# A second PSUM bank for the filler matmuls, and Mish as four products of 1024 columns

## The chip, the core and the metric

One core of one Trainium2 chip runs the whole program. The metric is device time in microseconds from launch to end. Before the change it is 889.89 us, the median of three runs (887.64 to 893.85).

## What is computed

The reference is one block with two branches over the same 2048 x 640 input, mixed by a gate per row (bfloat16 in and out):

```python
def _A_ref(x, wqkv, wo):                      # 32 heads of 20 columns
    q, k, v = ...                             # x @ wqkv
    scores = einsum("bhqd,bhkd->bhqk", q, k) * 20 ** -0.5
    o = einsum("bhqk,bhkd->bhqd", softmax(scores), v)
    return o @ wo
def _B_ref(x, w1, b1, w2):                    # 640 -> 1536 -> 640
    h = x @ w1 + b1
    return (h * tanh(softplus(h))) @ w2       # Mish
g = sigmoid((x * gate_w).sum(-1, keepdims=True))
return g * _A_ref(x, ...) + (1 - g) * _B_ref(x, ...)
```

The work that sets the scale is the exponential of 32 x 2048 x 2048 scores.

## The kernel before, in words

The kernel is a program that plans its own instruction streams. `attention()` walks through steps; at each step it appends instructions to a list, and each engine (TensorE, called pe; ScalarE, act; VectorE, dve; GpSimd, pool; SyncE, sp) later runs its part of that list in order, with semaphores where one waits for another. A planner's clock with costs such as `EXP`, `WIDE`, `PASS` decides what fits where; the order is fixed before the chip runs.

**Steps.** The scores are cut into 2048 blocks of 128 keys x 512 queries (the last group of one quarter of the queries in two halves of 256). A step handles a slot of up to three blocks. TensorE writes them into three of the eight PSUM banks: even steps into banks 0 to 2, odd steps into banks 3 to 5 (`scores(s)`). The score matmuls (L1045) use 32 rows of the array each, so the two or three of one step run beside one another and cost one pass of 512 columns. ScalarE then takes the exponential of the whole slot in one instruction (`emit_e`, L1068) from PSUM into `ETS`. In many steps the third block goes to VectorE instead: `choose` hands it over, `emit_x` (L1099) forms an int16 whose bits are an approximate fp16 exponential, and three shaded copies (L1119) are made of each finished tile of four blocks, so that each such tile is summed from four shades. ScalarE's instruction then covers only two blocks (1024 columns). The scores of step s+2 are issued while ScalarE is at step s+1 (`emit_s(step + 2)`), and need the banks that step s has left.

**Value products.** Four finished blocks are multiplied with V (L1224), four matmuls beside one another, accumulating in bank 6 (`ACC`); a group ends with a copy to `OUNG` and a division by the sums that goes through a DRAM round trip (L1295 to L1305, L1265).

**Fillers.** All other matmuls are tasks: keys, queries and values (L536 to L711), the bound on the scores (L752), the hidden layer (`h_task`, L829), its output (`b_task`, L900), the output projection (`p_task` and `part_task`, L924). `pick` takes the next task whose inputs are ready, `put` issues one of its matmuls at a time, at most up to the planned end of ScalarE's instruction (`limit` in the main loop), and all use bank 7 (`FB`): a new task waits until VectorE has emptied the bank of the one before. What has not found a place by the last step is issued after it.

**Mish.** Pairs of finished hidden tiles (1024 columns) go to ScalarE for a tanh (L863) and then to VectorE in twelve pieces (L879 to L893): a square, a sum, a product, a product of halves, a reciprocal (L883), and products with it. The pieces lie in a queue (`blend`) and are slipped in wherever `work` finds room on VectorE.

**The end.** After the last step the remaining fillers run, then eight last projections of the last 256 queries (`late_mm`), their mixing and the stores.

## Time and profile before

| | before |
|---|---|
| median of 3 runs | 889.89 us (887.64 to 893.85) |
| the profiled execution's own time | 890.57 us |
| its span, first to last instruction | 888.0 us |
| TensorE busy (matmul rows) | 774.3 us, 87% |
| ScalarE busy | 799.7 us, 90% |
| VectorE busy | 734.8 us, 83% |
| mean granted TensorE clock | 0.981 of full speed |

The page has a busy sum for each engine, the span in forty slices, the chain of work that ended last, and groups of instructions with what ended the idle time before them. Busy is the union of an engine's rows: a matmul's row goes on after the next one may start, so a busy TensorE is not one without room. The time of one step of a pipelined engine is therefore read from start to start in the rows in order of time.

### The profile page before, as it was taken

The numbers are of one execution on the slowest core, as the hardware profiler recorded it, in microseconds if no ns is written. First come the engines' busy times: TensorE is split into PE (matmuls) and PEld (weight loads), VectorE is DVE, ScalarE is ACT, GpSimd is POOL, SyncE is SP. The second block draws the span as 40 slices with busy tenths as digits, with TensorE's granted clock in tenths as the row PEclk, the third lists the DMA queues.
The fourth block names the chain that finished last, engine by engine and source line by source line (L and its number), as shares of the span: only waits on it lengthen the run. The fifth ranks groups of instructions, "written<-read, shape, count | busy, mean of one in ns | idle before, by whom it ended". The sixth has DMA issues, their size and how long they took to land.

```text
span 888.0 us, 17316 instructions
## 1 busy us (share of the span) xinstructions
PE 774.3 (87%) x7304; PEld 275.8 (31%) x7304; DVE 734.8 (83%) x1232; ACT 799.7 (90%) x714; POOL 16.4 (2%) x29
## 2 busy tenths in 40 slices
PE   7887898989899888979999989889999899888874
PEld 3333233223432223212223323333333333333332
DVE  4785787799978889988789888999999989878753
ACT  6987987999789997969999999999999999999930
POOL 2000000000000000000000000000000000000000
PEclk9998999999999999979999999999999999999997
DMA  9012010001112211121111112111011202111101
GB/s 215 19 43 61 29 55 16 13 28 53 52 37 72 65 45 44 44 65 47 42 45 34 40 54 66 44 43 54 18 36 50 77 14 72 50 44 51 35 12 34
DMA packets 70021, 42.57 MB, mean 48 GB/s; under 512 B 20616, under 2 KB 65920, under 8 KB 69888
## 3 DMA queue, kind: packets, MB, share of 16 engines
q1 hardware_dynamic: 67568, 40.89, 16.4%
q8 instruction: 60, 0.98, 0.5%
q10 hardware_dynamic: 2256, 0.47, 0.3%
q0 software_dynamic: 112, 0.01, 0.1%
q14 instruction: 25, 0.20, 0.1%
HBM read 33.97 MB, written 5.23 MB: 44 GB/s over the span
## 4 chain that ended last, share of the span: by engine, by line
ACT 73%; PE 14%; DVE 6%; DMA 6%; issue 1%; SPq 0%
ACT ETS L1068 71%; PE PS L1224 4%; PE PS L1045 3%; DMA KT<-KS 3%; DMA KS<-LN 2%; PE PS L536 2%; ACT REG L863 2%; PE PS L924 1%; DVE LN L1099 1%; PE PS L711 1%; PE PS L900 1%; DVE LN L1119 1%; PE PS L590 1%; DMA LN<-in_A_x_dram 1%; DMA SUMS<-RR 1%
## 5 line engine op out<-in xcount | busy, mean ns | idle before, releaser
L1068 ACT ACTIVATE ETS<-PS 128x1536 bf16<-128x1536 f32 (+1 forms) x683 | 783.3, 1418 | 46.3 <-PE PS L1045 38.9
L1045 PE MATMUL PS<-QT,KT 32*128 32x512 bf16 (+1 forms) x2146 | 271.0, 380 | 83.3 <-ACT ETS L1068 62.8
L1099 DVE TENSOR_SCALAR LN<-PS 128x512 int16<-128x512 f32 x276 | 185.9, 684 | 33.1 <-PE PS L1045 30.8
L1224 PE MATMUL PS<-ETS,V_all 128*21 128x512 bf16 (+1 forms) x1764 | 168.8, 380 | 0.1
L1045 PEld LDWEIGHTS PS<-QT,KT 32*128 32x128 bf16 x2146 | 67.6, 91 | 296.4 <-ACT ETS L1068 267.3
L1119 DVE TENSOR_SCALAR LN<-LN 128x2048 int16<-128x2048 int16 x163 | 107.8, 682 | 2.9 <-PE PS L1224 2.8
L1224 PE MATMUL PS<-LN,V_all 128*21 128x512 f16 x1132 | 98.8, 390 | 0.6 <-DVE LN L1119 0.6
L900 PE MATMUL PS<-W2R,HB 128*128 128x320 bf16 x384 | 72.5, 302 | 2.5 <-DVE XB L907 2.4
L1224 PEld LDWEIGHTS PS<-ETS,V_all 128*21 128x21 bf16 x1764 | 42.6, 90 | 77.2 <-issue 68.5
L829 PE MATMUL PS<-XB,REG 128*128 128x256 bf16 x360 | 56.2, 275 | 1.4 <-DVE OUTT L930 0.7
L924 PE MATMUL PS<-WOQ,QT 128*128 128x320 bf16 x256 | 50.3, 310 | 8.0 <-DVE W2R L930 5.2
L536 PE MATMUL PS<-XB,WOQ 128*128 128x512 bf16 x155 | 45.3, 391 | 1.9 <-DVE HB L839 0.8
L900 PEld LDWEIGHTS PS<-W2R,HB 128*128 128x128 bf16 x384 | 30.1, 97 | 38.8 <-issue 25.2
L839 DVE TENSOR_TENSOR HB<-PS,B1F 128x512 bf16<-128x512 f32 x48 | 33.0, 687 | 11.0 <-PE PS L829 10.4
L883 DVE RECIPROCAL T<-T 128x256 f32<-128x256 f32 x24 | 41.9, 1744 | 0.1
L829 PEld LDWEIGHTS PS<-XB,REG 128*128 128x128 bf16 x360 | 29.0, 97 | 28.2 <-issue 26.0
L1224 PEld LDWEIGHTS PS<-LN,V_all 128*21 128x21 bf16 x1132 | 22.4, 90 | 42.8 <-issue 24.7
L548 DVE CAST QT<-PS 128x512 bf16<-128x512 f32 x31 | 21.3, 686 | 14.4 <-PE PS L536 14.1
L924 PEld LDWEIGHTS PS<-WOQ,QT 128*128 128x128 bf16 x256 | 20.3, 99 | 34.3 <-issue 13.2
L1295 DVE COPY OUNG<-PS 128x512 f32<-128x512 f32 x31 | 21.2, 684 | 8.1 <-PE PS L1224 7.9
L1585 ACT ACTIVATE LN<-PS,GATE 128x320 f32<-128x320 f32 x1 | 0.5, 528 | 29.4 <-PE PS L924 29.4
L863 ACT ACTIVATE REG<-HB 128x1024 f32<-128x1024 bf16 x18 | 25.4, 1413 | 0.0
(123 smaller groups left out, 607.9 us busy)
## 6 DMA issues: line engine op xcount, KB each, us to landing
REG<-in_B_w_dram SPq DMA_DIRECT2D x36, 320.0 KB, 3.2
BCT<-SUMS SPq DMA_DIRECT2D x31, 256.0 KB
W2R<-in_B_w_dram SPq DMA_DIRECT2D x12, 320.0 KB, 4.8
KT<-KS SPq DMA_DIRECT2D x28, 128.0 KB
KS<-LN SPq DMA_DIRECT2D x16, 128.0 KB, 2.5
W2R<-in_B_w_dram SPq DMA_DIRECT2D x1, 1920.0 KB, 8.6
out_dram<-OUTT SPq DMA_DIRECT2D x24, 80.0 KB, 1.6
REG<-in_A_wqkv_dram SPq DMA_DIRECT2D x2, 700.0 KB, 8.5
```

Of the source, the lines that this page charges most:

```text
L536: return lambda e, bank: e.matmul(PS[:, bank, :], pads[:, b, f, :], xt(c)[:, f, :], start=(f == 0), stop=(f == NFT - 1))
L829: return lambda e, bank: e.matmul(PS[:, bank, i * HW:(i + 1) * HW], w1b(n1)[:, f, i * P:(i + 1) * P], xt(c)[:, f, cols], start=(f == 0), s ...
L839: ev = dve(lambda e: e.tensor_tensor(hb, PS[:, bank, :].rearrange("p (i t) -> p i t", i=2), bias, ALU.add), [last, *b1f, *guarded, *b_read ...
L863: ex = pl.add("act", lambda e: e.activation(U, h, AF.Tanh, scale=0.5), [ev, u_free[0]], cost=0.95)
L883: piece(RECIP, lambda e: e.reciprocal(T1[:, :], T1[:, :]))
L900: return lambda e, bank: e.matmul(PS[:, bank, 0:HALF], HB[:, hc % 2, f, t * P:(t + 1) * P], W2[:, f, half * HALF:(half + 1) * HALF], start ...
L924: return lambda e, bank: e.matmul(PS[:, bank, 0:HALF], otn(c, g)[:, t * P:(t + 1) * P], WOG[:, g, half * HALF:(half + 1) * HALF], start=(g ...
L1045: op = pl.add("pe", lambda e, i=i, g=real(g), tile=tile, j=j, cols=cols, c=c, of_q=of_q: e.matmul(scores(s)[:, i, cols], KT[32 * j:32 * j ...
L1068: e_op[s] = pl.add("act", lambda e: e.activation(ETS[:, s % NETS, 0:n, :], scores(s)[:, 0:n, :], AF.Exp, scale=SCALE), [s_op[s], pv_slot.g ...
L1099: ev_op[s] = tile["op"] = dve(lambda e: e.tensor_scalar(dst, scores(s)[:, 2, :], SCALE * ULPS, BASE, ALU.mult, ALU.add), [s_op[s], *tile[" ...
L1119: op = pl.add("dve", lambda e: e.tensor_scalar(to, src, SHADES[n], None, ALU.add), [last, *deps], cost=SHADE)
L1224: lasts[n] = pl.add("pe", lambda e, tile=tile, h=real(g) * HG + j, j=j, src=src[:, cols], of_q=of_q, begin=begin, end=end: e.matmul(PS[32 ...
```

## The change

1. `lend()`: from step 2 on, while the planner's filler rate is above `LEND`, an odd step's slot holds two blocks instead of three (`compose`, `n = SLOT - ...`), and its third bank, 5, is lent to the fillers as `SECOND`. `home()` takes for each new task the one of banks 7 and 5 that came free first. No block goes to VectorE in such a step (`choose` is not asked).
2. The number of steps is no longer fixed; the loop runs until all blocks are done, and due times go by the share of blocks issued (`now["at"]`).
3. `limit` is raised by `OVER` = 0.233: a filler may end that much after the planned end of ScalarE's instruction.
4. Mish: tanh with a bias (`BEND`, from a column of `MXR`), then four products of 1024 columns, without reciprocal. `U2` doubles, `T1` goes, `OUTT` moves into `REG`.
5. Some twenty constants of the planner are other numbers; the tasks' due times end 83 slots before the last instead of 45.

The diff, cut to this:

```diff
-SLACK = 0.3
-LATER = 0.9
+SLACK = 0.21
+LATER = 0.616
...
-END = 45
-SHIFT = 0.4
+END = 83
+SHIFT = 0.492
...
-                ex = pl.add("act", lambda e: e.activation(U, h, AF.Tanh, scale=0.5), [ev, u_free[0]], cost=0.95)
+                G = U2[:, :]
+                ex = pl.add("act", lambda e: e.activation(U, h, AF.Tanh, bias=MXR[:, 3:4], scale=0.5),
+                            [ev, u_free[0], m_bias], cost=0.95)
...
-                piece(RECIP, lambda e: e.reciprocal(T1[:, :], T1[:, :]))
...
+                a, b, c = QUART
+                piece(BROAD, lambda e: e.scalar_tensor_tensor(G, U, a, U, ALU.add, ALU.mult))
+                piece(BROAD, lambda e: e.scalar_tensor_tensor(U, U, 1.0, h, ALU.add, ALU.mult))
+                piece(BROAD, lambda e: e.scalar_tensor_tensor(G, G, b, G, ALU.add, ALU.mult))
+                piece(BROAD, lambda e: e.scalar_tensor_tensor(h, G, c, U, ALU.add, ALU.mult), done)
...
+            n = SLOT - (s % 2 and now["lent"])
             if extra:
-                slots[s] = [order.popleft(), order.popleft(), extra]
+                slots[s] = [order.popleft() for _ in range(min(n - 1, len(order)))] + [extra]
             else:
-                slots[s] = [order.popleft() for _ in range(min(SLOT, len(order)))]
+                slots[s] = [order.popleft() for _ in range(min(n, len(order)))]
+            now["at"] = (len(units) - len(order)) // SLOT - 2
...
+        def lend():
+
+            if now["open"] and now["home"] == SECOND:
+                return
+            want = fast and now["step"] > 1 and now["rate"] > LEND
+            if want and not now["lent"]:
+                s = now["step"]
+                bank_free[SECOND] = ev_op[s] if s in off else e_op[s] if len(slots[s]) == SLOT else bank_free.get(SECOND)
+            now["lent"] = want
...
+        def home():
+
+            some = [FB, SECOND] if now["lent"] else [FB]
+            return min(some, key=lambda n: bank_free[n].t1 if bank_free.get(n) is not None else 0.0)
...
-            limit = pl.now["act"] + (EXP_PAIR if fast and step + 1 in off else EXP) + HOP if step < NSLOT else 1e9
+            limit = pl.now["act"] + wide(step + 1) + HOP + OVER if busy else 1e9
```

What the change moves, at three places.

TensorE in the middle of the loop, about where the first output projections are placed (L1045, now L1048: scores; L1224, now L1242: value products; L924, now L925, and L829, now L840: fillers). Before:

```order
L1045 MATMUL PS<-QT,KT 128x512 x3
L924 MATMUL PS<-WOQ,QT 128x320 x3
L1045 MATMUL PS<-QT,KT 128x512 x3
L1224 MATMUL PS<-ETS,V_all 21x512 x4
L924 MATMUL PS<-WOQ,QT 128x320
L1045 MATMUL PS<-QT,KT 128x512 x3
```

The same stretch of the changed program:

```order
L1048 MATMUL PS<-QT,KT 128x512 x3
L840 MATMUL PS<-XB,REG 128x256
L925 MATMUL PS<-WOQ,QT 128x320 x3
L1048 MATMUL PS<-QT,KT 128x512 x2
L1242 MATMUL PS<-ETS,V_all 21x512 x4
L925 MATMUL PS<-WOQ,QT 128x320
L1048 MATMUL PS<-QT,KT 128x512 x3
```

Every second score set has two matmuls instead of three, and one task's last matmul is followed at once by the next task's first (an L840, then L925), in the other bank. Over the whole program there are 817 score sets instead of 683 and 797 value sets instead of 773; the fillers are the same (546,640 columns of moving data in all); and the stream changes from one of the three kinds (score, value, filler) to another 1883 times instead of 1574, 573 of them from filler to score instead of 454.

TensorE at the end of the program. Before, from the last score set on:

```order
L1045 MATMUL PS<-QT,KT 128x256 x4
L924 MATMUL PS<-WOQ,QT 128x320 x4
L1224 MATMUL PS<-ETS,V_all 21x256 x8
L900 MATMUL PS<-W2R,HB 128x320 x5
L1224 MATMUL PS<-ETS,V_all 21x256 x8
L900 MATMUL PS<-W2R,HB 128x320 x43
L924 MATMUL PS<-WOQ,QT 128x320 x56
L1481 MATMUL PS<-KT 128x512
L924 MATMUL PS<-WOQ,QT 128x320 x8
```

The changed program, from its last score set on (L1506 is an idle pass that no result uses):

```order
L1048 MATMUL PS<-QT,KT 128x256 x6
L1242 MATMUL PS<-ETS,V_all 21x256 x8
L925 MATMUL PS<-WOQ,QT 128x320 x2
L1242 MATMUL PS<-ETS,V_all 21x256 x16
L1506 MATMUL PS<-KT 128x512 x5
L925 MATMUL PS<-WOQ,QT 128x320 x8
```

The 43 and 56 filler matmuls that followed the last value set stand ahead of it now; behind it are only the eight last projections and idle passes.

VectorE, one Mish pass among its other work. Before, its later half:

```order
L883 RECIPROCAL T<-T 128x256
L1119 TENSOR_SCALAR LN<-LN 128x2048
L839 TENSOR_TENSOR HB<-PS,B1F 128x512
L884 TENSOR_TENSOR U<-U,T 128x512
L1119 TENSOR_SCALAR LN<-LN 128x2048
L888 TENSOR_TENSOR REG<-REG,U 128x256 x2
L891 SCALAR_TENSOR_TENSOR REG<-REG,U 128x256
L839 TENSOR_TENSOR HB<-PS,B1F 128x512
L891 SCALAR_TENSOR_TENSOR REG<-REG,U 128x256
L892 SCALAR_TENSOR_TENSOR HB<-REG,HB 128x512
L893 SCALAR_TENSOR_TENSOR HB<-REG,HB 128x512
```

The changed program, from a pass's second product to its fourth (L1117: a block's approximate exponential; L1137: a shade):

```order
L892 SCALAR_TENSOR_TENSOR REG<-REG,HB 128x1024
L1137 TENSOR_SCALAR LN<-LN 128x2048
L1117 TENSOR_SCALAR LN<-PS 128x512
L1320 RECIPROCAL RR<-RR 128x16
L893 SCALAR_TENSOR_TENSOR U<-U 128x1024
L1117 TENSOR_SCALAR LN<-PS 128x512
L1137 TENSOR_SCALAR REG<-LN 128x2048
L908 TENSOR_SCALAR XB<-PS,OMG 128x320
L1117 TENSOR_SCALAR LN<-PS 128x512
L894 SCALAR_TENSOR_TENSOR HB<-U,REG 128x1024
```

There are 24 passes in both; a pass has four instructions of 1024 columns instead of twelve of 256 to 1024. VectorE now takes 380 blocks instead of 348 (L1117) and makes 285 shades instead of 261 (L1137). ScalarE has 34 exponentials of 1536 columns and 783 of 1024, before 334 and 349. The DMA issues keep their number and kinds.

## Rows read from the trace of the kernel before

**Rows 1.** Page: busy us of each engine, share of the span, instructions.
```profile
PE 774.3 (87%) x7304; PEld 275.8 (31%) x7304; DVE 734.8 (83%) x1232; ACT 799.7 (90%) x714; POOL 16.4 (2%) x29
```

**Rows 2.** Windows: stretch, busy of each engine (instructions), clock, DMA share, GB/s.
```profile
10.00:450.00 440.00, 386.00 (x3760) 133.62 (x3754) 361.50 (x609) 394.06 (x361) 11.26 (x19) 0.97 0.18 49
450.00:852.00 402.00, 360.92 (x3387) 128.62 (x3385) 356.42 (x591) 401.79 (x348) 0.00 (x0) 1.00 0.16 45
852.00:888.00 36.00, 20.34 (x121) 10.19 (x121) 11.70 (x23) 0.88 (x2) 0.86 (x1) 0.86 0.08 23
```

**Rows 3.** Waits of ScalarE, 10 to 450 us: total us, times, longest.
```profile
ACT ETS L1068 <- PE PS L1045: 38.9, 35, 2.9
ACT ETS L1068 <- PE PS L1224: 6.7, 2, 3.5
```

**Rows 4.** Timeline at the end: start us, us, engine, line, names, count, idle.
```profile
843.87 8.48 ACT L1068 ACTIVATE ETS<-PS 128x1536 bf16<-128x1536 f32 x6
...
854.35 0.42 DVE L1288 TENSOR_TENSOR QT<-PS,BCT 128x256 bf16<-128x256 f32 x1
...
855.29 1.80 PE L900 MATMUL PS<-W2R,HB 128*128 128x320 bf16 x12 [1.14 <-DVE XB L907]
...
880.19 2.34 PE L924 MATMUL PS<-WOQ,QT 128*128 128x320 bf16 x8
```

**Rows 5.** Timeline of ScalarE, 768.41 to 782 us.
```profile
768.41 12.52 ACT L1068 ACTIVATE ETS<-PS 128x1536 bf16<-128x1536 f32 x9
780.39 1.48 ACT L863 ACTIVATE REG<-HB 128x1024 f32<-128x1024 bf16 x1
781.34 1.88 ACT L1068 ACTIVATE ETS<-PS 128x1536 bf16<-128x1536 f32 x1
```

**Rows 6.** Timeline of ScalarE, 303.6 to 309 us.
```profile
303.14 5.69 ACT L1068 ACTIVATE ETS<-PS 128x1024 bf16<-128x1024 f32 x6
308.56 1.20 ACT L863 ACTIVATE W2R<-HB 128x1024 f32<-128x1024 bf16 x1
```

**Rows 7.** Timeline, 606 to 610.4 us, TensorE.
```profile
608.29 0.39 PE L1045 MATMUL PS<-QT,KT 32*128 32x512 bf16 x3 [0.20 <-ACT ETS L1068]
...
608.62 0.40 PE L1224 MATMUL PS<-LN,V_all 128*21 128x512 f16 x4
...
608.84 0.39 PE L1224 MATMUL PS<-REG,V_all 128*21 128x512 f16 x4
...
609.16 0.50 PE L829 MATMUL PS<-XB,REG 128*128 128x256 bf16 x3
...
609.64 0.39 PE L1045 MATMUL PS<-QT,KT 32*128 32x512 bf16 x3
```

**Rows 8.** Groups of VectorE by shape: names, shapes, count, busy us, mean ns, idle.
```profile
L1099 DVE TENSOR_SCALAR LN<-PS 128x512 int16<-128x512 f32 x276 | 185.9, 684 | 33.1 <-PE PS L1045 30.8
L1119 DVE TENSOR_SCALAR LN<-LN 128x2048 int16<-128x2048 int16 x163 | 107.8, 682 | 2.9 <-PE PS L1224 2.8
L883 DVE RECIPROCAL T<-T 128x256 f32<-128x256 f32 x24 | 41.9, 1744 | 0.1
...
L879 DVE SCALAR_TENSOR_TENSOR REG<-REG 128x1024 f32<-128x1024 f32 x18 | 21.9, 1216 | 2.1 <-ACT REG L863 2.1
...
L888 DVE TENSOR_TENSOR REG<-REG,U 128x256 f32<-128x256 f32 x36 | 15.1, 419 | 0.5
...
L892 DVE SCALAR_TENSOR_TENSOR HB<-REG,HB 128x512 bf16<-128x512 f32 x18 | 12.3, 685 | 0.2
```

**Rows 9.** Waits of TensorE, 10 to 450 us: total us, times, longest.
```profile
PE PS L1045 <- ACT ETS L1068: 29.0, 97, 1.1
PE PS L1045 <- DMA KT<-KS: 7.2, 5, 3.7
```

**Rows 10.** Windows around the first fall of the clock.
```profile
78.00:82.00 4.00, 0.42 (x5) 0.22 (x6) 0.98 (x2) 1.08 (x1) 0.00 (x0) 1.00 0.77 187
82.00:86.00 4.00, 3.42 (x42) 2.11 (x46) 2.78 (x5) 2.40 (x2) 0.00 (x0) 0.54 0.06 14
```

More of the change, by code (lines that the diff above doesn't have):

```diff
@@ L342, in attention @@
         acts = deque()
-        now = {"step": -1, "open": None, "bank": False, "rate": 9.0}
+        now = {"step": -1, "at": -2, "open": None, "home": FB, "bank": False, "rate": 9.0, "lent": False}
         if fast:
@@ L387, in later, with dve @@
             at.setdefault(step, []).append(fn)
-        def dve(fn, deps=(), cost=0.1, kind="F"):
+        def dve(fn, deps=(), cost=0.1, kind="F", slack=SLACK):
             ready = max([pl.now["dve"], *(d.t1 + HOP for d in deps if d is not None)])
-            work(ready + (LATER if fast and now["rate"] < BUSY and now["bank"] else SLACK))
+            work(ready + (LATER if fast and now["rate"] < BUSY and now["bank"] else slack))
             return pl.add("dve", fn, deps, cost=cost, kind=kind)
@@ L1424, in pick @@
             for t in tasks:
-                if begin + t.cost > limit or passed and t.due > now["step"] + EAGER:
+                if begin + t.cost > limit or passed and t.due > now["at"] + EAGER:
                     return None
@@ L1456, in room @@
         def room():
[L1458 removed]
+            step = now["at"]
             if step < start:
@@ L1493, in fill_up @@
                     spin(FB, free)
-                elif short and not idle and step + 2 < NSLOT and pl.now["pe"] + PASS + TAIL["pe"] + HOP <= upto:
+                elif short and not idle and step + 2 in slots and pl.now["pe"] + PASS + TAIL["pe"] + HOP <= upto:
                     repeat_s(step + 2)
@@ L1499, in attention @@
         owed = 0.0
-        for step in range(NSLOT + 40):
+        step = -1
+        while True:
+            step += 1
             now["step"] = step
-            if step >= NSLOT and not queue and not tasks and not any(k >= step for k in at):
-                break
-            for t in [t for t in tasks if t.forced and t.due <= step]:
+            assert step < 1500, (len(order), len(tasks), len(queue))
+            if not order and step not in slots:
+                now["at"] = max(now["at"] + 1, NSLOT)
+                if not queue and not tasks and not any(k >= step for k in at):
+                    break
+            for t in [t for t in tasks if t.forced and t.due <= now["at"]]:
                 while now["open"] not in (None, t):
@@ L1513, in attention @@
                 load_w2()
-            if acts and safe(acts[0][0]) < pl.now["act"] and mish_free():
+            if acts and (safe(acts[0][0]) < pl.now["act"] and mish_free() or step not in slots and u_free[0] != "busy"):
                 acts.popleft()[1]()
@@ L1517, in attention @@
             rate = behind = 0.0
-            lag = max((step - t.due for t in tasks if not t.forced and t.ready() is None), default=0)
+            lag = max((now["at"] - t.due for t in tasks if not t.forced and t.ready() is None), default=0)
             for t in tasks:
-                slack = max(1, t.due - AHEAD * t.forced - step)
+                slack = max(1, t.due - AHEAD * t.forced - now["at"])
                 ahead += t.left()
@@ L1526, in attention @@
             now["rate"] = rate
-            if step + 2 < NSLOT:
-                able = step >= CALM and (step < slot_of(0, 1, 0) or behind < CATCH_UP and lag < LAG and room())
-                compose(step + 2, choose(step + 2, able) if fast else None)
+            if order:
+                able = now["at"] >= CALM and (now["at"] < slot_of(0, 1, 0) or behind < CATCH_UP and lag < LAG and room())
+                if step % 2:
+                    lend()
+                compose(step + 2, choose(step + 2, able) if fast and not (step % 2 and now["lent"]) else None)
                 emit_s(step + 2)
@@ L1550, in attention @@
                 fn()
-            work(pl.now["act"] + 0.5 if step < NSLOT else 1e9)
+            work(pl.now["act"] + 0.5 if busy else 1e9)
         assert not queue and not tasks and not bg and not soon and not norm and not tile_now[0] and not blend and not acts, (len(queue), len(tasks), len(bg), len(acts))
```

106 lines of the change are left out of this document (54 added, 52 removed).

## The prediction

> **What bounds the kernel now.** I read the busy sums first [rows 1]: ScalarE 799.7, TensorE 774.3, VectorE 734.8 us of 888, so no average names a bound. The table of stretches does [rows 2]. From 450 to 852 us ScalarE is busy 401.79 of 402 us: there the exponentials are the bound, and nothing else matters. From 10 to 450 us it is busy 394.06 of 440, and the table of its waits says for whom it stood: 45.6 us, nearly all for a score matmul [rows 3]. From 852 us on it does nothing (0.88 us), and neither does much else: TensorE 20.34 of 36 us. The timeline of the end shows what runs there [rows 4]: ScalarE's last exponential is over at 843.87 + 8.48 = 852.35; the last division is done at 854.35 + 0.42 = 854.77; the eight last projections, which need only that, start at 880.19. Between the two stand filler matmuls, one task at a time in one bank: twelve run 1.80 us and then wait for VectorE to empty it.
>
> So the 890.57 us of the profiled execution (0.7 above the median of 889.89) are:
> - 10.0 before the first exponential;
> - the loop, 842.35, in which ScalarE's own work is priced from start to start: nine of 1536 columns from 768.41 to 780.39, 1.331 each; a tanh to 781.34, 0.95 [rows 5]; six of 1024 from 303.14 to 308.56, 0.903 each [rows 6]. 334 x 1.331 + 349 x 0.903 + 24 x 0.95 = 782.5. With the 45.6 of waits 14.2 are left, exponentials that run a little longer than these;
> - 35.65 behind the last exponential, and 2.57 outside the span.
>
> **The change, part by part.**
>
> *The end.* In the changed order the 43 + 56 fillers stand ahead of the last value set; behind it are idle passes and the eight projections. They can start at 854.77 instead of 880.19 of before's clock: 25.4 us less, 35.65 becomes 10.2. It holds if the loop has room for these fillers, which is the next question. The idle passes (five of 0.22) lie beside VectorE's division.
>
> *ScalarE.* 34 x 1.331 + 783 x 0.903 + 24 x 0.95 = 775.1, that is 7.4 less: 32 more blocks go to VectorE (32 x 0.428, the difference of the two prices, 13.7), and 134 more instructions cost their fixed part, 0.903 - 2 x 0.428 = 0.047, or 6.3. The Trainium skill (ScalarE: Activation LUTs, What ACT_TABLE_LOAD costs) speaks against short instructions more strongly: 186 ns fixed with 93 ns overlapped when back to back, so 93 ns for each, and by that the 134 would cost 12.5 us, an estimate from that page, and the sum 6 us more; the rows of this kernel read from PSUM and show about half, and decide. The same section gives 93 ns more for an operand that is a pointer; tanh now has its bias from a column, 24 x 0.093 = 2.2 us as an estimate, and no row here shows it.
>
> *VectorE.* A Mish pass was one of 1.216, one reciprocal of 1.744, four of 0.685 and six of 0.419 us [rows 8], 8.21; now it is four of 1.216 (the same kind of instruction on 1024 columns), 4.86. 24 x 3.35 = 80.4 less. 32 x 0.684 for blocks and 24 x 0.682 for shades are 38.3 more. 734.8 - 80.4 + 38.3 = 692.7, or 86% of a loop of some 808 us, as dense as before (717.9 of 842). Lower bound of the new pass: these rows overlap by a little, so nothing is lost there. Upper bound: 1.744 for each, were the mixed bfloat16 operand slow; then 734.8 + 8.9, 92%: tight, not the bound. Cost on the path: none, hidden by ScalarE's work; what it brings is only the room for the extra blocks.
>
> *TensorE.* This is where the change is paid. Prices [rows 7]: a set of value products follows another after 0.22 (608.62 to 608.84); where the kind changes it is 0.33 (score to value, 608.29 to 608.62) or 0.32 (608.84 to 609.16), so a change costs 0.105; from a narrow filler to a score it is more: three of 256 columns take 0.33 by 0.22 for 512, and the score came after 0.48 (609.16 to 609.64), 0.15, though some of this may be waiting. A score set of two costs the same pass as one of three. So:
> - before: (683 + 773) x 0.22 + 546,640 columns x 0.22/512 + 1574 x 0.105 = 320.3 + 234.9 + 165.3 = 720.5; with 0.05 more on 454 filler-to-score changes 743;
> - after: (817 + 797) x 0.22 + 234.9 + 1883 x 0.105 = 355.1 + 234.9 + 197.7 = 787.7; with 0.05 on 573, 816.
>
> Of this 99 fillers of 320 columns (13.6) lay behind the loop before, and 2.2 do now. In the loop TensorE's load was 707 to 730 of 842, 84 to 87%; now it is 785 to 814 against ScalarE's 775.1 + 14.2 = 789. The two are level. That is the main uncertainty: ScalarE would wait between nothing and 25 us for TensorE alone.
>
> *Waits.* What eases them: a filler in the second bank need not wait for VectorE, and the forced key and query tasks are spread. What the overrun risks: a score set that starts late. A two-block step lasts 0.903; two steps give 1.81 for the way from one exponential through the score set of two steps on to the next, of which a score set takes 0.33 and its drain some tenths, so an overrun of 0.233 is just covered. Before, TensorE stood 29.0 us of the first 450 for ScalarE and 7.2 for keys from DRAM [rows 9]; the key loads are the same 28. I take waits of W = 20 us, within 0 to 25 nearer the upper end, because TensorE's true price lies between mine and any stand of it now counts. Bounds: 0 as in 450 to 852, and 46 as in the whole loop before.
>
> *Small edits.* A memset of one column and the new home of the output tile hide in the start and in stores that nothing waits for. The DMA issues keep their number, so SP's queue is as before.
>
> **Sum.** 10.0 + 775.1 + 14.2 + W + 10.2 + 2.57 = 812.1 + W. With W = 20: **832 us**, 7% below 889.89.
>
> **The rivals.**
> - *TensorE rules.* For: 816 by the dearer price is above ScalarE's work. Against: the dearer price has waiting in it. W is then 25, the key loads' 7.2, and half of the 29 that it stands for ScalarE: 46, and the time 858.
> - *No waits.* For: 402 us of before without one. Against: TensorE had 13% of room there. W = 0: 812, and with a third of the 14.2 gone 808.
> - *The granted clock, slower.* Before, TensorE had a wait of nearly 4 us (busy 0.42 of 4 us at 78 to 82) and the clock stood at 0.54 in the next window [rows 10], that is mostly at 1.2 GHz; the mean of 0.97 over the first 440 us [rows 2] makes 26 us at that level. Passes and columns, 590 of some 808 us, double at 1.2 GHz, so each such microsecond costs about 0.7. To lose the 58 us of the sum it needs about 83 us at 1.2 GHz beside what there was; with 100 the time is 902. The place is the loop, wherever DRAM or VectorE holds a score set. Against: TensorE now pauses less than before. The Trainium skill (TensorE: Matmul & The Clock Gate, A second HAM failure mode: psum-queue depth-cycling) tells of a kernel that cycles through PSUM banks and whose short pauses between groups let the clock swing; by that rule this kernel with one more bank to cycle would lose clock. The trace of before disagrees so far: it cycles seven banks and holds 1.00 from 450 to 852.
> - *VectorE holds the banks.* A product of 1.216 cannot be broken off, so the block's evacuation in an even step may be late and its three banks too. For: 86% load. Against: before it had a 1.744 reciprocal and TensorE's wait for it is not among the large ones. If each of 96 products held a score set by 0.5 us: 48 more, 880.
>
> **How the numbers follow.** The likeliest, 832 (W from 8 to 35: 820 to 847), 0.58; TensorE rules, 858, 0.20; no waits, 812, 0.12; the banks held, 880, 0.06; the clock, 902, 0.04. The range, 808 to 858, leaves out the last two and the far side of the second. About 1% is what a measurement of this kernel can tell from no change, so faster means under 881: 0.58 + 0.20 + 0.12 and half of the banks' 0.06, 0.93; same 0.03; slower 0.04.
>
> **What would show it.** Right: ScalarE's last exponential ends near 820, and the span some 10 us later, with no fillers between the division and the eight projections; ScalarE busy near 795; TensorE's waits for ScalarE far under the 29.0 of before's first 450 us alone; VectorE near 693 with 1.2 us for each of the 96 products; the clock at 0.97 or above. Wrong: waits of ScalarE for scores above 35 us, spread over the whole span (TensorE rules) or in a few long ones with the clock low behind them (the clock); a wait of the score matmuls for L1117 of tens of microseconds (the banks); fillers behind the last exponential.

## The result, and the profile after

The changed kernel takes 854.59 us (median of 4 runs, 852.54 to 858.33) beside 891.87 for the kernel before in the same comparison: ratio 0.959, 95% interval 0.952 to 0.965. The direction is right and the range of 808 to 858 holds the time, but the likeliest case, 832, is missed by 22.6 us. What came is close to the time that the prediction gave to the rival "TensorE rules", 858.

The page of the changed kernel: busy sums, the granted clock over the span in 40 slices, and the chain of work that ended last.

```profile
span 850.2 us, 17518 instructions
PE 832.1 (98%) x7405; PEld 286.0 (34%) x7405; DVE 701.8 (83%) x1097; ACT 817.7 (96%) x848; POOL 15.2 (2%) x29
PEclk9999999999999999999999999999999999999999
PE 86%; ACT 10%; DMA 2%; SPq 1%; issue 0%; DVE 0%
PE PS L1048 32%; PE PS L1242 24%; ACT ETS L1086 9%; PE PS L901 7%; PE PS L840 7%; PE PS L547 5%; PE PS L925 4%; PE PS L722 2%; PE PS L601 2%; DMA XB<-in_A_x_dram 1%; SPq L478 1%; PE PS L763 1%; DMA REG<-in_B_w_dram 1%; PE PS L695 1%; PE PS 
```

TensorE went from 774.3 us of 888 [rows 1] to 832.1 of 850, and the chain now runs through it for 86% of the span, 32% being score matmuls (L1048); before, the loop's second half was ScalarE's alone. The clock is 9 tenths or more in every slice. The stretches that answer to [rows 2] (columns: span of the stretch, then busy time and instruction count of TensorE's matmuls, its weight loads, VectorE, ScalarE and GpSimd, then the clock):

```profile
10.00:450.00 440.00, 435.79 (x3875) 145.40 (x3869) 345.10 (x554) 430.94 (x446) 10.27 (x20) 1.00 0.19 53
450.00:820.00 370.00, 366.13 (x3164) 127.31 (x3160) 331.90 (x496) 362.24 (x378) 0.00 (x0) 1.00 0.15 44
```

Before, ScalarE was busy 401.79 of 402 us from 450 us on; now it has gaps all through the loop, and TensorE has 99% from the start. The waits of ScalarE, though, are few (columns: engine, line, whom it waited for: us in total, times, longest), against 38.9 and 6.7 us in the first 450 us of before [rows 3]:

```profile
ACT ETS L1086 <- PE PS L1048: 8.5, 34, 1.1
ACT LN L1624 <- PE PS L925: 2.5, 1, 2.5
ACT ETS L1086 <- PE PS L1242: 1.1, 3, 0.5
```

Nor did TensorE wait for others (5.3 us for ScalarE in the whole span, by 29.0 in 440 us of before [rows 9], and nothing named for the key loads). **Where are ScalarE's waits, then?** In the groups by shape, first of before, then of after (columns: count, busy, mean ns of one, and idle before them):

```profile
L1068 ACT ACTIVATE ETS<-PS 128x1024 bf16<-128x1024 f32 x349 | 340.1, 1151 | 31.3 <-PE PS L1045 23.9 <-PE PS L1224 6.7
```

```profile
L1086 ACT ACTIVATE ETS<-PS 128x1024 bf16<-128x1024 f32 x783 | 748.9, 1028 | 16.5 <-PE PS L1048 8.0 <-PE PS L1242 1.1
L1086 ACT ACTIVATE ETS<-PS 128x1536 bf16<-128x1536 f32 x34 | 48.8, 1466 | 0.5 <-PE PS L1048 0.5
L874 ACT ACTIVATE REG<-HB,MXR 128x1024 f32<-128x1024 bf16 x18 | 20.6, 1144 | 0.0
```

An exponential of 1024 columns took 1151 ns on the mean before and 1028 after, although it is the same work. Rows of successive exponentials overlap: six took 0.903 us each from start to start [rows 6], 0.25 less than one such row is long. An exponential that was not ready ahead of time has a shorter row: those of after that start more than 0.95 us behind the start of the one before are 1.02 us long. So a lateness of up to 1.02 - 0.90 = 0.12 us books no idle time; only the overlap shrinks. The starts show what the waits do not. Over 735 pairs of neighbours of 1024 columns in after, 299 start more than 0.95 us after the one before, 258 of them between 0.95 and 1.15 us; the lateness of the 299 beyond 0.904 sums to 47.2 us. Of this, 16.5 us stand as idle time in the group above and 9.6 in the waits: 142 of the 299 have no gap before them, and 121 one of at most 0.15 us, which the table of waits leaves out. Before, it is 51 of 293 pairs, and 19 long ones (over 1.5 us) carry 32.4 of their 39.8 us. So ScalarE was held up rarely and long before, and is held up often and briefly now.

The end, in order of time (start, busy, engine, line, count, and in brackets the idle before):

```profile
834.65 6.43 ACT L1086 ACTIVATE ETS<-PS 128x1536 bf16<-128x1536 f32 x5
841.46 1.25 PE L1506 MATMUL PS<-KT 128*128 128x512 bf16 x5
842.78 0.42 DVE L1306 TENSOR_TENSOR QT<-PS,BCT 128x256 bf16<-128x256 f32 x1
843.60 0.53 ACT L1624 ACTIVATE LN<-PS,GATE 128x320 f32<-128x320 f32 x1 [2.53 <-PE PS L925]
```

The last exponential ends at 834.65 + 6.43 = 841.08; idle passes (L1506) fill the division, no filler is left, and the span ends 9.1 us later, where before 35.65 us lay behind it [rows 4]. The whole sum of after, in its own profiled execution (852.54 us): 10.3 to the first exponential, 830.8 for the loop, 9.1 behind it, 2.3 outside the span.

### The profile page after: what moved, and what is told of

Read it like the earlier page. It is cut to its first block, busy times and chain, and to the rows that moved or that the text cites. A ratio compares the mean times of both kernels' runs of the same rounds, so it can differ in the third digit from the quotient of the medians.

```text
span 850.2 us, 17518 instructions
## 1 busy us (share of the span) xinstructions
PE 832.1 (98%) x7405; PEld 286.0 (34%) x7405; DVE 701.8 (83%) x1097; ACT 817.7 (96%) x848; POOL 15.2 (2%) x29
## 4 chain that ended last, share of the span: by engine, by line
PE 86%; ACT 10%; DMA 2%; SPq 1%; issue 0%; DVE 0%
PE PS L1048 32%; PE PS L1242 24%; ACT ETS L1086 9%; PE PS L901 7%; PE PS L840 7%; PE PS L547 5%; PE PS L925 4%; PE PS L722 2%; PE PS L601 2%; DMA XB<-in_A_x_dram 1%; SPq L478 1%; PE PS L763 1%; DMA REG<-in_B_w_dram 1%; PE PS L695 1%; PE PS L620 0%; ACT REG L874 0%
## 5 line engine op out<-in xcount | busy, mean ns | idle before, releaser
L1086 ACT ACTIVATE ETS<-PS 128x1024 bf16<-128x1024 f32 (+1 forms) x817 | 791.8, 1047 | 17.0 <-PE PS L1048 8.5
L1048 PE MATMUL PS<-QT,KT 32*128 32x512 bf16 (+1 forms) x2112 | 357.4, 377 | 6.6 <-ACT ETS L1086 5.3
L1117 DVE TENSOR_SCALAR LN<-PS 128x512 int16<-128x512 f32 x300 | 206.2, 687 | 72.8 <-PE PS L1048 68.4
L1242 PE MATMUL PS<-ETS,V_all 128*21 128x512 bf16 (+1 forms) x1720 | 163.7, 377 | 1.0 <-ACT ETS L1086 0.9
L1048 PEld LDWEIGHTS PS<-QT,KT 32*128 32x128 bf16 x2112 | 81.7, 91 | 230.6 <-ACT ETS L1086 130.5
L1137 DVE TENSOR_SCALAR LN<-LN 128x2048 int16<-128x2048 int16 x183 | 122.4, 684 | 0.5
L1242 PE MATMUL PS<-LN,V_all 128*21 128x512 f16 (+1 forms) x1300 | 111.8, 377 | 0.0
L901 PE MATMUL PS<-W2R,HB 128*128 128x320 bf16 x384 | 76.9, 303 | 0.0
L1242 PEld LDWEIGHTS PS<-ETS,V_all 128*21 128x21 bf16 x1720 | 42.1, 89 | 73.7 <-issue 64.3
L840 PE MATMUL PS<-XB,REG 128*128 128x256 bf16 x360 | 58.1, 275 | 0.4 <-DMA REG<-in_B_w_dram 0.4
L925 PE MATMUL PS<-WOQ,QT 128*128 128x320 bf16 x256 | 52.4, 303 | 0.0
L901 PEld LDWEIGHTS PS<-W2R,HB 128*128 128x128 bf16 x384 | 30.0, 97 | 44.7 <-issue 38.8
L1242 PEld LDWEIGHTS PS<-LN,V_all 128*21 128x21 bf16 x1300 | 25.9, 89 | 52.9 <-issue 27.8
L840 PEld LDWEIGHTS PS<-XB,REG 128*128 128x128 bf16 x360 | 28.6, 97 | 30.0 <-issue 26.4
L1117 DVE TENSOR_SCALAR REG<-PS 128x512 int16<-128x512 f32 x44 | 30.2, 686 | 7.5 <-PE PS L1048 6.7
L925 PEld LDWEIGHTS PS<-WOQ,QT 128*128 128x128 bf16 x256 | 20.2, 97 | 29.6 <-issue 25.3
L893 DVE SCALAR_TENSOR_TENSOR U<-U 128x1024 f32<-128x1024 f32 x24 | 29.0, 1210 | 0.0
L722 PE MATMUL PS<-REG,XB 128*128 128x160 bf16 (+1 forms) x240 | 26.0, 234 | 0.0
```

The source lines that it names most:

```text
L722: return lambda e, bank: e.matmul(PS[:, bank, i * n:(i + 1) * n], xt(t // 4)[:, f, t % 4 * P:(t % 4 + 1) * P], WV[:, f, g * HD:g * HD + n] ...
L840: return lambda e, bank: e.matmul(PS[:, bank, i * HW:(i + 1) * HW], w1b(n1)[:, f, i * P:(i + 1) * P], xt(c)[:, f, cols], start=(f == 0), s ...
L893: piece(BROAD, lambda e: e.scalar_tensor_tensor(G, G, b, G, ALU.add, ALU.mult))
L901: return lambda e, bank: e.matmul(PS[:, bank, 0:HALF], HB[:, hc % 2, f, t * P:(t + 1) * P], W2[:, f, half * HALF:(half + 1) * HALF], start ...
L925: return lambda e, bank: e.matmul(PS[:, bank, 0:HALF], otn(c, g)[:, t * P:(t + 1) * P], WOG[:, g, half * HALF:(half + 1) * HALF], start=(g ...
L1048: op = pl.add("pe", lambda e, i=i, g=real(g), tile=tile, j=j, cols=cols, c=c, of_q=of_q: e.matmul(scores(s)[:, i, cols], KT[32 * j:32 * j ...
```

## What the missing 22 us are

The loop was to take 775.1 + 14.2 + 20 = 809 us and took 830.8. TensorE in the middle of the loop of after, in order of time; the count is that of matmuls, the number ahead of the engine the busy time:

```profile
510.76 0.60 PE L1048 MATMUL PS<-QT,KT 32*128 32x512 bf16 x3
511.30 0.58 PE L901 MATMUL PS<-W2R,HB 128*128 128x320 bf16 x3
511.81 0.39 PE L1048 MATMUL PS<-QT,KT 32*128 32x512 bf16 x2
512.13 0.40 PE L1242 MATMUL PS<-ETS,V_all 128*21 128x512 bf16 x4
512.45 0.45 PE L901 MATMUL PS<-W2R,HB 128*128 128x320 bf16 x2
512.83 0.39 PE L1048 MATMUL PS<-QT,KT 32*128 32x512 bf16 x3
513.15 0.40 PE L1242 MATMUL PS<-REG,V_all 128*21 128x512 f16 x4
```

Two score sets of three stand here. That at 512.83 is followed after 0.32, one pass of 0.22 and a change of kind. That at 510.76 is followed after 0.54: **two** passes. They differ in the heads of their blocks. A score matmul sits on the strip of 32 rows of its head:

```python
scores(s)[:, i, cols], KT[32 * j:32 * j + 32, g, ...], QT[32 * j:32 * j + 32, g, ...], tile_position=(32 * j, 0)
```

Three blocks of heads 0, 1 and 2 lie on three strips and run beside one another. If two of the three have the same head j, they want the same strip, and the second runs behind the first. I counted the heads in both programs: before, no score set has two blocks of one head (11 of the 683 sets are issued again as idle work, 12 passes in all); in the changed order 189 of 817 have, every one of them a set of three in an even step, and the double is the block that VectorE takes. Over the whole trace of after, 187 of the 189 take 0.50 to 0.60 us from their start to the start of what follows, and 617 of the other 628 less than 0.40. The prediction said that a score set costs one pass whatever it holds. With the second passes its own tally reads

(817 + **189** + 797) x 0.22 + 234.9 + 1883 x 0.105 = 829.3 us

(2.2 of it behind the loop) for a loop that took 830.8. The Trainium skill (TensorEngine Tiling (Array Packing), Key Properties) says that tiles of the array work independently and that *different* tiles can run matmuls in parallel. It does not say what two matmuls on one tile do; the trace shows them one behind the other, 0.54 by 0.32 us. I had not asked of the changed order which tiles its sets use.

That was a theory from one trace. The experiments ask which engine bounds the loop, what each part of the change brings alone, and whether the second passes are the cause.

## Which engine bounds the loop

**Less work for ScalarE.** Every exponential leaves out 32 of its 512 columns per block (those hold a constant, so the output is not the reference's); the order stays.

```diff
...
-ETS[:, s % NETS, 0:n, :], scores(s)[:, 0:n, :], AF.Exp, scale=SCALE),
+ETS[:, s % NETS, 0:n, 0:CW - 32], scores(s)[:, 0:n, 0:CW - 32], AF.Exp, scale=SCALE),
```

> The changed kernel with one edit: each exponential leaves out the last 32 columns of its blocks, which hold ones instead; the order is the same. ScalarE loses 64 columns in 783 instructions and 96 in 34, at 0.428 us for 512: 783 x 0.0535 + 34 x 0.080 = 44.6 us. Theory T: nothing comes off, or the little that ScalarE still made TensorE wait, 845 to 856. Theory H: half, 828 to 840. Theory A: 810 to 815.

Measured: 852.20 us (849.29 to 855.66), by 854.59 of the changed kernel. Some 45 us of ScalarE's work were taken away and about 2 came back; in the profiled execution the clock stood at 1.2 GHz for 10 us (26 to 36 us), and the fastest run, with a mean clock of 1.00, was 849.29. The page, and ScalarE's waits:

```profile
PE 90%; ACT 4%; DMA 3%; SPq 1%; issue 1%; DVE 1%; DVEq 0%
```

```profile
ACT ETS L1088 <- PE PS L1050: 25.6, 85, 1.6
```

ScalarE waits more and the loop is no shorter: TensorE sets its length.

**Less work for TensorE.** The fillers of L901 move 64 of their 320 columns (384 matmuls; the rest of their output is left out).

```diff
-PS[:, bank, 0:HALF], HB[...], W2[:, f, half * HALF:(half + 1) * HALF],
+PS[:, bank, 0:64], HB[...], W2[:, f, half * HALF:half * HALF + 64],
```

> The changed kernel with one edit: the matmuls of the hidden layer's output (L901) move 64 columns instead of 320, so four fifths of that product are left out; the order on every engine is the same. TensorE loses 384 x 256 columns, at 0.22 us for 512 of them 42 us. Theory T (TensorE's own work bounds the loop, 98% busy): most of it comes off until ScalarE's work bounds, 854.6 - 30 to 42, so 813 to 825. Theory H (the two engines are held by each other's latency, each score set by an exponential and back): the hold stays, 838 to 848. Theory A (ScalarE bounds): 852 to 857.

Measured: 876.08 and 883.37 us in two runs, 898.24 and 900.19 in two others at a lower clock, all slower than the changed kernel although nothing was added. Stretches of its profile (the run of 883.37) behind the place where the narrow fillers begin (375 us):

```profile
396.00:400.00 4.00, 3.77 (x40) 1.08 (x36) 3.89 (x7) 4.00 (x6) 0.00 (x0) 1.00 0.02 2
400.00:416.00 16.00, 15.28 (x136) 4.59 (x132) 10.74 (x19) 15.26 (x18) 0.00 (x0) 0.89 0.14 44
416.00:457.00 41.00, 40.31 (x244) 9.89 (x240) 24.32 (x37) 29.84 (x32) 0.00 (x0) 0.59 0.14 35
457.00:480.00 23.00, 23.00 (x183) 6.96 (x181) 16.54 (x29) 19.88 (x21) 0.00 (x0) 0.85 0.13 38
```

The clock, 1.00 until 406 us, fell to its lower level (1.2 GHz) for some 126 us in nine stretches. In the 4 us ahead of the first fall TensorE's rows were busy for 3.68, with score and value sets and the narrow fillers between them; the narrow fillers are the only edit. In these stretches the exponentials came 46 us later, in sum, than at 0.903 and 1.331 us from start to start; TensorE's work is only 42 us less. At the full clock they came earlier than in the changed kernel: from the same exponential on (375 us), 0.049 us late on the mean by 0.071 there. So a lighter TensorE eases the loop where the clock holds, but the total of this run says nothing on the bound. It shows the rival "the granted clock" at work, in another kernel than the one that it was put up for.

## The parts of the change, one by one

The planner's other constants stay as they are in the kernel that is edited, so a part alone runs with numbers that were set for another combination; what a part is worth holds for these kernels as they stand.

**No bank lent.** The overrun, Mish and the due times stay.

```diff
-            want = fast and now["step"] > 1 and now["rate"] > LEND
+            want = False
```

> The changed kernel without the lent bank: every slot has three blocks again, the rest (Mish, constants, overrun, due times) stays. 695 score sets and 827 value sets, 1598 changes of kind, 420 blocks for VectorE; ScalarE 262 x 1.331 + 421 x 0.903 + 25 = 754 us of its own; 91 fillers are left for after the last exponential, in one bank. Theory T: TensorE has 13% of room in the loop, so the loop comes near ScalarE's 754 + 14 and a few waits, and the end is 22 us longer: 810 to 835, faster than with lending. Theory H, and the forecast's own reading of what lending is for: fillers wait for their one bank and TensorE's bursts hold the scores, as before the change, 46 us of waits: 845 to 865.

Measured: 866.15 us (865.81 to 867.16), ratio 0.976 (0.973 to 0.979). ScalarE's waits:

```profile
ACT ETS L1086 <- PE PS L1048: 27.5, 24, 3.5
ACT ETS L1086 <- PE PS L1242: 26.1, 10, 4.3
ACT LN L1624 <- PE PS L925: 26.0, 1, 26.0
```

That is a microsecond above the higher of the two expectations. Its loop is 821.3 us, shorter than the changed kernel's 830.8, but fillers are left over and 32.0 us lie behind the last exponential instead of 9.1. So the lent bank empties the end, 23 us, and charges 10 of them to the loop (if anything more: 17 us of the loop without it ran at 1.2 GHz, none of the changed kernel's).

**Only Mish**, in the kernel before (the 12 pieces replaced by the four products and the bias; `MISH`, the planner's cost of a whole pass, stays at 3.6).

```diff
-                piece(RECIP, lambda e: e.reciprocal(T1[:, :], T1[:, :]))
...
+                piece(BROAD, lambda e: e.scalar_tensor_tensor(G, U, a, U, ALU.add, ALU.mult))
+                piece(BROAD, lambda e: e.scalar_tensor_tensor(U, U, 1.0, h, ALU.add, ALU.mult))
...
```

> The kernel before with the new Mish alone (four products, output tile in the other place; the planner's cost of a pass is left at the old figure). VectorE takes 376 blocks instead of 348: ScalarE 306 x 1.331 + 377 x 0.903 + 25 = 773, 10 less; but 140 fillers instead of 99 are left for the end, one at a time, some 8 us more. Theory of the parts (Mish alone brings nothing, the bank and the due times take the end away): 880 to 892. If Mish is what brings the gain: 850 to 870.

Measured: 897.71 us (896.83 to 900.93), ratio 1.010 (1.004 to 1.016): no gain, but a loss of 1%, 8.7 us.

```profile
ACT ETS L1062 <- PE PS L1039: 46.6, 44, 2.9
ACT LN L1579 <- PE PS L918: 36.3, 1, 36.3
```

VectorE falls from 734.8 to 700.3 us and takes 376 instead of 348 blocks, but the loop (843.1 us, 842.0 before) waits in a few long stops for scores as before, and more fillers are left at the end (42.3 us by 35.65). The room on VectorE was not what this kernel lacked.

**The old Mish in the changed kernel**: the same edit the other way round, on the lent bank.

```diff
+                piece(RECIP, lambda e: e.reciprocal(T1[:, :], T1[:, :]))
...
-                piece(BROAD, lambda e: e.scalar_tensor_tensor(G, U, a, U, ALU.add, ALU.mult))
-                piece(BROAD, lambda e: e.scalar_tensor_tensor(U, U, 1.0, h, ALU.add, ALU.mult))
...
```

> The changed kernel with the old Mish of twelve pieces (and its planner cost). VectorE is 80 us heavier, so the planner gives it 308 blocks instead of 380: ScalarE 103 x 1.331 + 716 x 0.903 + 23 = 806, TensorE (819 + 154 second passes + 743) x 0.22 + 235 + 1754 x 0.105 = 797, and 86 fillers are left for after the last exponential, 20 us. Mish matters through what it lets VectorE take: 855 to 875. If it does not matter: 850 to 857.

Measured: 885.97 us (881.29 to 889.76), ratio 0.995 (0.992 to 0.998), 31 us slower than the changed kernel and slower than expected. With the dearer pieces the planner hands VectorE 308 blocks instead of 380, and issues 135 idle passes on TensorE where it had 10: by the planner's clock, which has no second passes (154 here), TensorE stands idle there. The page shows TensorE as the greater part of the chain again, in a loop of 857.0 us with 19.5 behind it:

```profile
PE 842.7 (95%) x7214; PEld 294.3 (33%) x7278; DVE 696.8 (79%) x1163; ACT 840.5 (95%) x850; POOL 15.2 (2%) x29
PE 65%; ACT 29%; DVE 2%; DMA 1%; SPq 1%; issue 1%
```

The new Mish is thus worth 31 us beside the lent bank and nothing in the kernel before. Some 10 of them lie behind the loop; how the rest divide between idle passes, longer exponentials and the clock (0.77 from 10 to 40 us) I have not separated.

**No overrun.** This asks whether the overrun, which lets a filler delay the next score set, is where the 22 us went.

```diff
-OVER = 0.233
+OVER = 0.0
```

> The changed kernel with its overrun taken away: OVER = 0 instead of 0.233, nothing else. In its order 117 fillers are then left behind the last exponential, and 170 of the score sets still have two blocks of one head. Theory S (the second pass of such a set, 0.22 us each, and TensorE as the bound): TensorE's work in the loop is (820 + 170 + 767) x 0.22 + 234.9 - 13.6 + 1871 x 0.105 = 804 us, ScalarE's own 748 x 0.903 + 71 x 1.331 + 24 x 1.04 + 14.2 = 809; so level, with some 10 us of waits; behind the loop the fillers cost some 40 us as in the kernel before (35.7 for 99). 10 + 819 + 40 + 2.6 = 855 to 872 us, no faster than the changed kernel. Rival V (the overrun itself makes score sets late and is where the missing 22 us went): without it the loop is free of these waits, and the time is 832 to 845 us in spite of the fillers behind.

Measured: 876.75 us (875.47 to 884.13), ratio 0.989 (0.986 to 0.993).

```profile
ACT ETS L1086 <- PE PS L1048: 17.1, 23, 1.8
ACT ETS L1086 <- PE PS L1242: 11.9, 6, 3.1
ACT LN L1624 <- PE PS L925: 17.4, 1, 17.4
```

The rival is out: without the overrun the loop is 839.5 us, 9 longer, and the end 23.4, 14 longer. My number was low by 5, and it is two errors that nearly cancel: the loop was expected at 819, the end at 40.

**Fewer changes of kind.** The 1883 changes at 0.105 were the largest new term of TensorE's tally. Here value sets are issued only in odd steps and fillers only in even ones, which leaves 1538.

```diff
-            emit_pv(step, 2 if busy else 99)
+            emit_pv(step, (2 if step % 2 == 1 else 0) if busy else 99)
...
-            while owed > 0:
+            while owed > 0 and (not busy or step % 2 == 0):
```

With OVER at 0.3 and a longer account for the fillers (`owed` up to 2.0), all of them still find a place.

> The changed kernel with the planner's rule altered: value products only in odd steps, two sets one behind the other, fillers only in even steps, with an overrun of 0.3 instead of 0.233. The work is the same (817 score sets, 797 value sets, 380 blocks for VectorE), but TensorE's stream changes kind 1538 times instead of 1883. Theory T: 345 x 0.105 = 36 us less work for TensorE, until ScalarE bounds: 818 to 830. Theory H: longer runs of one kind hold the next score set longer, 850 to 870. Theory A: 852 to 857.

Measured: 870.85 us (870.46 to 873.28), 16 more than the changed kernel, though the changes of kind are 36 us less in the tally (the planner also issues 50 idle passes instead of 10, some 9 us). Waits of TensorE:

```profile
PE PS L1048 <- ACT ETS L1086: 26.2, 65, 1.6
PE PS L1048 <- DVE W2R L931: 4.4, 1, 4.4
```

A long run of one kind pushes the next score set back, and then TensorE waits in turn. 183 sets still had two blocks of one head. Bundling work in this way did not win the price of a change back.

## Taking the second passes away

**Half of them.** Where the block for VectorE has the head of one of the two blocks of its set, the set takes the other pair of the same four heads; the number of instructions of each kind stays, and 87 of the 189 second passes are left.

```diff
+                four = [order[i] for i in range(min(4, len(order)))]
+                js = [u[3] for u in four]
+                if (n == SLOT and len(four) == 4 and len({u[:3] for u in four}) == 1
+                        and extra[3] in js[:2] and extra[3] not in js[2:]):
+                    order.rotate(-2)
+                    slots[s] = [order.popleft(), order.popleft()]
+                    order.rotate(2)
+                    slots[s].append(extra)
```

> In the changed kernel 189 of the 817 score sets hold two blocks of the same head of their group (the block that goes to VectorE and one of the other two): both need the same 32 rows of the array, and the second runs behind the first. Here an even step takes the third and fourth of the next four blocks instead of the first and second where that avoids it; nothing else moves, and the number of instructions stays. 87 such sets are left. Theory S (those second passes are the time that the forecast missed): 102 x 0.22 = 22 us less, 828 to 838, as long as the clock holds. Theory K (the changes of kind and the hold between the engines are what was missed, the strips do not matter): 851 to 858. Should TensorE's lighter load let the clock fall as in the run with narrow filler matmuls: above 855, with long stretches at 1.2 GHz.

Measured: 840.19 us (836.38 to 841.52), ratio 0.945 (0.940 to 0.950), 14 less than the changed kernel, 2 above the expectation. The chain:

```profile
PE 52%; ACT 41%; DMA 2%; DVE 2%; SPq 1%; issue 1%
```

**All of them.** Beside that edit, a set gets a third block only where the four heads of a tile begin; elsewhere it keeps to two.

```diff
+            if fast and not extra and s % 2 == 0 and now["lent"] and order[0][3] == 0:
+                n = 2
...
-compose(step + 2, choose(step + 2, able) if fast and not (step % 2 and now["lent"]) else None)
+compose(step + 2, choose(step + 2, able) if fast and not (step % 2 and now["lent"]) and not (now["lent"] and order[0][3]) else None)
```

> As the run before, and even steps without a block for VectorE take two blocks instead of three while the bank is lent, so that the blocks stay in step with the groups of four: no score set holds two blocks of one head any more. 828 score sets, 1901 changes of kind. TensorE: 41.6 us less for second passes, 3.5 more for 11 sets. Theory S: its work comes to 831 - 38 = 793 us in the loop, level with ScalarE's 12 x 1.331 + 816 x 0.903 + 25 + 14 = 792, so 815 to 832. Theory K: 851 to 860. With the clock falling: above 840.

Measured: **829.77 us** (829.17 to 831.43), ratio 0.933 (0.928 to 0.938): 25 us faster than the changed kernel, and the fastest version of this study that leaves no work out. Its page, its exponentials by shape, and three score sets of three in the same place of the loop as above:

```profile
PE 796.9 (96%) x7367; PEld 286.1 (35%) x7409; DVE 696.0 (84%) x1097; ACT 797.7 (96%) x859; POOL 15.0 (2%) x29
ACT 66%; PE 28%; DMA 2%; DVE 2%; SPq 1%; issue 1%; DVEq 0%
```

```profile
L1097 ACT ACTIVATE ETS<-PS 128x1024 bf16<-128x1024 f32 x816 | 756.6, 1083 | 9.1 <-PE PS L1253 4.3 <-PE PS L1059 4.1
```

```profile
507.51 0.39 PE L1059 MATMUL PS<-QT,KT 32*128 32x512 bf16 x3
507.83 0.72 PE L840 MATMUL PS<-XB,REG 128*128 128x256 bf16 x5
...
509.35 0.39 PE L1059 MATMUL PS<-QT,KT 32*128 32x512 bf16 x3
509.67 0.72 PE L840 MATMUL PS<-XB,REG 128*128 128x256 bf16 x5
...
511.30 0.39 PE L1059 MATMUL PS<-QT,KT 32*128 32x512 bf16 x3
511.62 0.39 PE L840 MATMUL PS<-XB,REG 128*128 128x256 bf16 x2
```

Each of these sets is followed after 0.32 us, the chain is back on ScalarE, the mean row of an exponential is longer again (1083 ns by 1028), so more of them are ready ahead of time, and of 786 pairs of neighbours 87 start late instead of 299 of 735. The last exponential ends at 819.6 us, the "near 820" that the prediction gave for the changed kernel (841.1).

**Which engine bounds this version**: the same edit with the lighter exponentials of above (32 of 512 columns left out).

> The changed kernel with its score sets of two and three made up so that no set has two blocks of one head (as in the run of aligned sets, 829.8 us), and beside it every exponential 32 columns per block shorter (480 of 512), which takes about 45 us of ScalarE's work away; the columns left out hold a constant, so the output is not the reference's. What bounds the aligned kernel? Theory S: without second passes TensorE's own work is (830 + 797) x 0.22 + 234.9 + 1901 x 0.105 = 792 us and ScalarE's about 798, so the two are level, and a lighter ScalarE gains only what lies above TensorE: 812 to 826 us, with TensorE the greater part of the chain that ended last. Rival A (ScalarE alone is the bound, TensorE has room): 785 to 798. Rival W (waits of one for the other, whatever their loads): 827 to 832, no gain.

Measured: 823.53 us (822.23 to 827.66), 6 less than with whole exponentials. The chain is TensorE's again:

```profile
PE 79%; ACT 11%; DMA 4%; DVE 2%; SPq 1%; issue 1%; DVEq 0%
```

So the two engines are level in it, and a further gain needs both. Beside the first test of this kind the pair shows the size: with the lighter ScalarE, 852.20 us with 189 second passes and 823.53 without, 29 us, where 178 fewer passes and 18 more changes make 37 by the prices.

**More overrun** on the same version (OVER 0.3 for 0.233).

> The kernel of aligned sets (no score set with two blocks of one head) with OVER = 0.3 instead of 0.233, nothing else. Its numbers hardly move: 818 exponentials of 1024 and 12 of 1536 columns, 1925 kind changes instead of 1901, 23 idle passes instead of 14. Theory S (loads decide): TensorE + 3 x 0.22 + 24 x 0.105 = 3 us more, so 828 to 836 us, the same within what can be measured. Rival V (an overrun makes score sets late, so more of it costs): each of some 400 lent steps that start 0.067 us later would give up to 27 us, so 840 to 855 us.

Measured: 833.73 us (832.53 to 835.48), 4 us more, about the 3 that the counts make. More exponentials start late than with 0.233 (160 of 788 pairs, 24.7 us in sum, by 87 of 786, 18.6 us), so the longer overrun does delay some of them; all that it costs here is within the 4 us.

The loops, from the first exponential's start to the last one's end, beside the loads by the prices of the prediction (ScalarE's with the 14.2 and, but for before, with 1.04 for a tanh; TensorE's of before with the 12 repeated passes). TensorE's are those of the whole program: 13.6 of before's and some 2 of the others' lie behind the loop.

| kernel | sets with two blocks of one head | TensorE's load | ScalarE's load | loop | of the loop at 1.2 GHz | behind the loop |
|---|---|---|---|---|---|---|
| before | 0 | 723 | 796.7 | 842.0 | 23.9 | 35.7 |
| changed | 189 | 829.3 | 791.5 | 830.8 | 0 | 9.1 |
| changed, half of the second passes | 87 | 806.8 | 791.5 | 815.6 | 6.8 | 8.5 |
| changed, none | 0 | 792.0 | 792.0 | 809.6 | 16.9 | 9.0 |

With TensorE 38 us above ScalarE the loop is TensorE's load; with 15 it is 9 longer; where the two are level it is 18 longer. Of the 18, 9.0 are ten exponentials that came late while the clock stood at 1.2 GHz (24.4 to 27.8 and 806.1 to 819.7 us). That the rest is each engine waiting for the other is my reading; no run separates it.

## Why the prediction was right and wrong, point by point

- **The end**: 25.4 us were to go; 35.65 became 9.1, where 10.2 was said. Right, and for the reason given: the fillers found room in the loop. The bank did most of it, but not alone: 32.0 us lie behind the loop without it, 23.4 without the overrun and 19.5 with the old Mish.
- **ScalarE's own work**: right, but for the tanh, which the prediction had as an estimate and left out of its sum. Its time from start to start went from 0.95 [rows 5] to 1.04 us, 24 x 0.093 = 2.2 us. The Trainium skill (ScalarE: Activation LUTs, What ACT_TABLE_LOAD costs) gives 93 ns for a pointer operand; by that rule 0.947 becomes 1.040, and the trace agrees. Its 93 ns for each further back-to-back instruction do not fit the exponentials, which read PSUM: 0.903 holds between undisturbed ones, and 0.047 with it.
- **VectorE**: the products take 1.205 to 1.216 us each, as priced; the busy time is 701.8 for 692.7. The rows themselves sum to 761.2 instead of 802.0 before, 40.8 less where 42.1 were said; busy is their union, and they overlap by 59.5 us now instead of 67.2, which makes the other 8. (The upper bound of 734.8 + 8.9 should read 8.6.) As the row below shows, VectorE waits for TensorE now, not the other way round, so the rival of the held banks is out:

```profile
DVE LN L1117 <- PE PS L1048: 68.4, 112, 2.0
```

- **TensorE**: here is the step that failed. "A score set of two costs the same pass as one of three" took each set for one pass. 189 of them cost two, 41.6 us, and the load is 829.3 instead of 787.7. The other prices held: by the medians of the times from start to start in the loop of after, with 0.22 for a pass, a change of kind costs 0.09 to 0.11 us. The Trainium skill (TensorEngine Tiling (Array Packing), Key Properties) says that a change of tiling mode drains the engine; the trace agrees in that each change costs about 0.10 us, and does not show whether a drain is what takes it. The dearer 0.15 from filler to score, which the prediction kept in its upper end, does not come back in after (0.09 to 0.10), so it was waiting for the most part. Its upper end of 814 was therefore high for a wrong reason and still too low.
- **Waits**: W was 20 and came out as 830.8 - 775.1 - 2.2 - 14.2 = 39. But 20 was made for engines that are level, and without the second passes, where they are, the term is 809.6 - 792.0 = 18. That looks like the 20, but 9.0 of the 18 are the clock, which W did not contain: the waits proper are about half of what was said, and the agreement is in part luck.
- **The rival that came**: "TensorE rules" named the engine, the time and the chain, but not the mechanism. Its 46 us were the dearer change, key loads and half of TensorE's waits for ScalarE. Of these nothing came: 5.3 us of waits for ScalarE, none named for keys. That the range of 808 to 858 held the time is therefore in good part luck: its upper end was built from terms that stayed out, and the 41.6 us that came were in none.
- **The signs**: of those for being right, the empty end, the waits of TensorE for ScalarE (5.3) and the clock came; the last exponential came at 841.1 instead of near 820, and ScalarE was busy for 817.7 instead of 795. The sign for the rival was badly chosen: "waits of ScalarE for scores above 35 us". The waits show 9.6 of 47.2 us of lateness, because some of it vanishes in the overlap of two rows and some in gaps too short for that table. The chain (86%) and the mean row of an exponential (1028 by 1151 ns) tell it.
- **The clock**: 1.00 in both stretches and 0.991 in the slowest run, 858.33 us; the rival did not come. The prediction had weighed the Trainium skill (TensorE: Matmul & The Clock Gate, A second HAM failure mode: psum-queue depth-cycling) and read from it that one more bank to cycle would lose clock; this trace has 0.999 as the mean. It is no test of that rule, though: both kernels write all eight banks, and the change only gives bank 5 from the score sets to the fillers.

## What to carry to other kernels

When small matmuls are packed side by side in the array, count for each set which strips its members sit on: two on one strip are two passes, and a change that only reorders can make hundreds of such sets without adding an instruction. Price a reordered stream from the new order's own operands, not from the number of its sets. To see which of two pipelined engines holds the other, compare start-to-start times and the mean length of a row with an undisturbed one; idle time misses a delay that only shortens the rows' overlap.

## What I had not expected of the hardware

- Two matmuls of 512 columns on one strip of 32 rows run one after the other: 0.54 us to the next kind by 0.32 for a set on different strips, and 187 of 189 such sets like it.
- With the fillers of one line cut from 320 to 64 columns TensorE's clock fell to 1.2 GHz for some 126 us, the first time behind 4 us in which its rows were busy for 3.68; less work cost more time, 876 to 900 by 854.59 us.
- An exponential of 1024 columns that is late by up to 0.12 us behind its predecessor shows as a shorter row (1.02 by 1.15 us), not as idle time.
